# Loading the first q and k blocks as float32 pairs of blocks, and laying the steps anew

## The chip, the cores and the metric

The kernel runs on one core of a Trainium2 chip. The metric is the device time of one execution in microseconds (us). Instructions run on TensorE (PE, with its weight loads PEld), VectorE (DVE), ScalarE (ACT) and GpSimd (POOL); DMAs are issued by SyncE (SP), ACT and GpSimd.

## The reference

Sliding-window attention with a few global keys and a linear bias by distance, then a two-layer feed-forward network (FFN) with a softplus. Batch 4, 8 heads, 768 tokens, head size 64; 8 global keys, a window of 96; the FFN goes from 512 to 2048 and back to 512, over 3072 tokens.

```python
scores = scale * np.matmul(q, k.transpose(0, 1, 3, 2))
is_global = pos[None, :] < 8
is_local = (rel >= 0) & (rel < 96)
dist = np.where(is_global & ~is_local, 96.0, np.abs(rel))
scores = scores - slopes[:, None, None] * dist
scores = np.where(is_global | is_local, scores, -1e9)
a = softmax(scores)                     # with the row maximum taken off
x = np.matmul(a, v)                     # then heads side by side: (3072, 512)
h = x @ w_in
g = np.maximum(h, 0.0) + np.log1p(np.exp(-np.abs(h)))
out = g @ w_out
```

## The kernel before

The 3072 tokens are cut into 24 blocks of 128 (six to a batch) and 12 chunks of 256 for the FFN. A window of 96 reaches at most into the block before, so block n needs the keys and values of blocks n and n-1; the global keys of a batch's first block are copied over the first columns of the previous block's keys and values (gk and gv).

There is no loop that sets the order. A long string, ORDER, lists the steps one by one, each a short name with numbers, and KINDS maps a name to a function. Every engine runs its own instructions in the order in which the string emits them, so a step that waits holds up whatever its engine has behind it. A second string, BANKS, gives the PSUM bank (one of three) of each any_bank tile in the order of allocation.

The steps that matter here:

- lq, lk, lv: loads of a block's q, k, v by GpSimd's queue, from float32 in HBM to bf16 in SBUF. A single block is read in runs of 256 bytes (64 float32 of one head and token). For n in PAIRED (line 119), load_pair (line 124) reads two blocks in one DMA: partition s gets tokens 2s and 2s+1, in runs of 512 bytes. Before the change PAIRED holds 2 only.
- Block 0 is loaded differently (lines 87 to 92): as float32 into q_f by SP's queue and k_f by ACT's queue. cq (line 843) casts q to bf16 on DVE; ck (line 846) casts half of k on DVE and half on ACT.
- Transposes: t (line 275) of a block's q and k, four 128x128 transposes each; tq and tk (lines 851, 856) the same for block 0; tQ and tK (tr_pair, line 280) 16 half-width ones for the q or k of a pair. qc and kc copy the results from PSUM to QT and KT, on DVE, or on ACT when the last number is 1. For pairs these copies also interleave even and odd tokens. Later blocks are transposed by DMA (d).
- bb: parts of the bias table on ACT. z: the bias multiplied into PSUM by the identity, for blocks 0 to 3. s: the scores of half the heads, e: the exponential on ACT, p: the product with v, nm: the division on DVE, x and xc: the transpose to XT and its copy (y: by DMA).
- f, fe, lp, o: FFN of chunks 0 and 1, written as plain products. From chunk 2 on both layers use a seven-product scheme on quarters (h, hc, hv, he, hl; m, ec, ev, gs), with sums of weights made once (hw, wd). wi and wo load weights on GpSimd's queue. st stores by SP's queue.
- The last chunk's product m11.2 is cut in two column parts at LW (line 683); st11.0 is stored in the same two parts.
- g: a tiny copy on GpSimd that waits for a finished G, so that what stands behind it on GpSimd is issued later.

The beginning of ORDER before, in which w18 is 9 dummy matmuls that keep TensorE running until data is there:

```python
lk1 cq0 w18 bb1.0 lq1 z0.1 lq2 ck0 tq0 lv0 bb1.1 z0.0 tk0 s0.1 e0.1 lk2 s0.0 t1 kc1.0
lv1 qc1.0 lk4 z1.1 tQ2 s1.1 bb0.1 qc2.0 lq4 p0.1 e0.0 qc3.0 bb0.0 lv2 e1.1 p0.0 z1.0 wi1
```

Of the kernel before, what the change touches and what calls it, by code (L numbers as in the profile page):

```python
# [20 lines left out]
def kernel(  # L21
# [11 lines left out]
    nc = tc.nc  # L33
# [85 lines left out]
    PAIRED = (2,)  # L119
# [77 lines left out]
    def bias_part(half, part):  # L197
# [8 lines left out]
        "01201201022012012012012010120120120020012000102202001010200212201010222001102001"  # L206
        "122102021220110121210112020112020110"
# [475 lines left out]
    LW = 64  # L683
# [59 lines left out]
    def gate(s):  # L743
# [5 lines left out]
        lk1 cq0 w18 bb1.0 lq1 z0.1 lq2 ck0 tq0 lv0 bb1.1 z0.0 tk0 s0.1 e0.1 lk2 s0.0 t1 kc1.0  # L749
        lv1 qc1.0 lk4 z1.1 tQ2 s1.1 bb0.1 qc2.0 lq4 p0.1 e0.0 qc3.0 bb0.0 lv2 e1.1 p0.0 z1.0 wi1  # L750
        s1.0 lv3 nm0.0 tK2 e1.0 wi3 p1.1 lq5 gk2.1 lk5 wi0 nm0.1 kc2.0 p1.0 z2.0 z2.1 s2.1 x0
        s2.0 nm1.1 kc3.1 t4 gv2.0 gk3.0 nm1.0 e2.1 x1 z3.1 e2.0 lv4 wi2 qc4.1 z3.0 xc0.1 xc1.0
        s3.0 s3.1 kc4.0 p2.0 nm2.0 p2.1 nm2.1 f1 gv3.2 e3.0 p3.0 gk4.0 wi4 e3.1 x2 fe1 p3.1
        xc2.1 s4.0 gv4.1 f3 nm3.0 nm3.1 x3 ab4.0 t5 wo0 fe3 xc3.0 e4.0 s4.1 f9 lv5 ab4.1 kc5.1
        wi6 qc5.1 wo1 f11 fe9 e4.1 fe11 f8 gk5.2 f0 fe8 p4.0 s5.0 fe0 f10 ab5.0 lp0 nm4.0 hw1.0
        fe10 f2 s5.1 p4.1 f4 gv5.2 fe2 ab5.1 e5.0 f12 wo2 lp1 f5 o0 nm4.1 lq6 p5.0 hw2.0 o4 e5.1
        lk6 fe12 wo3 lk7 hw3.0 nm5.0 lq7 wd1.0 lp4 fe5 gv13 p5.1 fe4 x4 nm5.1 f13 xc4.0 x5 lp5
        hw3.1 fe13 f6 lp6 fe6 gs1.3 xc5.0 lq8 f14 f7 fe14 wd1.1 hw1.1 f15 h2.1.0 fe7 ht2.1 hw2.1
        o5 h2.5.0 fe15 lk8 ht2.2 hw4.1 lv6 lv7 hc2.1.0.1 ht2.4 hw4.0 h2.2.0 lp3 o1 lp2 h2.6.0
        wd3.0 o6 gv12 gk12 he2.11.0 hc2.5.0.0 wd2.0 lp7 hv2.6.0 wd4.0 ht2.3 gs1.1 t6 qc6.1 kc6.0  # L760
        h2.3.0 o2 o7 he2.12.0 hl2.0.0 wd3.1 lq9 os0.1.1 gs1.2 h2.7.0 ss6 t7 g7 hv2.7.0 ab6.0
        e6.0 o3 h2.4.0 os0.0.1 ac6.1 he2.21.0 qc7.0 kc7.0 lk9 wd2.1 ss7 ac6.0 gk8.2 m1.1.0 d8
        he2.22.0 ab7.0 e6.1 p6.0 h2.5.1 h2.1.1 ec1.1.1 lk11 hc2.5.1.1 ac7.0 hc2.1.1.1 lk10 g15
        e7.0 m1.6 nm6.0 p6.1 h2.2.1 lq10 h2.6.1 ec1.6.1 ac7.1 he2.11.1 m1.2.1 nm6.1 x6 p7.0
        wd4.1 hv2.6.1 h2.3.1 gs1.4 ev1.2 d9 e7.1 st0.1 nm7.0 xc6.1 h2.7.1 st0.0 hv2.7.1 ss8 d10
        gk9.2 he2.12.1 lv8 hl2.1.0 hl2.0.1 p7.1 ab8.0 m1.7 ac8.0 nm7.1 h2.4.1 h3.1.0 ec1.7.1
        lq11 m1.4 lv9 ac8.1 he2.21.1 hc3.1.0.1 x7 xc7.0 h3.2.0 gs2.3 ss9 e8.0 ec1.4.1 he3.11.0
        ht3.1 he2.22.1 e8.1 ac9.0 lq12 m1.5.0 ht3.2 ac9.1 ev1.5 h3.5.0 gv8.2 h3.6.0 lk12 p8.0
        ht3.4 m1.3 hc3.5.0.1 h3.1.1 ht3.3 hv3.6.0 nm8.0 d11 g21 e9.1 h3.3.0 ev1.3 p8.1 ab9.0
        hl2.1.1 he3.12.0 hc3.1.1.1 h3.7.0 m2.1.0 h3.2.1 e9.0 gk10.2 hv3.7.0 he3.11.1 nm8.1  # L770
        ec2.1.1 lv10 gv9.2 gs2.1 h3.4.0 p9.0 lq15 he3.21.0 h3.6.1 nm9.0 h3.5.1 hc3.5.1.1 p9.1
        hl3.0.0 lk13 ss10 gs2.2 he3.22.0 m2.6 gk11.2 nm9.1 hv3.6.1 h3.3.1 ec2.6.1 he3.12.1
        ab10.0 e10.0 y8 ac10.1 hl3.0.1 h3.7.1 y9 ac10.0 hv3.7.1 m2.7 d12 lv11 gv10.2 ec2.7.1
        ss11 p10.0 lq13 ac11.1 h4.1.0 h3.4.1 ac11.0 nm10.0 e10.1 ht4.1 m2.4 lk15 he3.21.1 ab11.0
        hc4.1.0.1 m2.2.1 h4.5.0 gs2.4 ht4.2 p10.1 gv11.0 ec2.4.1 ev2.2 he3.22.1 g27 m2.5.0 lq14
        ev2.5 lk14 hc4.5.0.1 d13 h4.6.0 ht4.3 hv4.6.0 e11.0 h4.2.0 hl3.1.0 he4.11.0 m2.3 h4.7.0
        ss12 nm10.1 ht4.4 p11.0 y10 ev2.3 lv13 hv4.7.0 nm11.0 e11.1 hl3.1.1 g23 d14 ac12.0 g13
        h4.3.0 gs3.1 ac12.1 h4.4.0 he4.12.0 p11.1 h4.1.1 m3.1.0 he4.21.0 hc4.1.1.1 gs3.2 nm11.1
# [64 lines left out]
    def cast_q(n):  # L843
        nc.vector.tensor_copy(q_t[n], q_f)
# [68 lines left out]
```

## Time and profile before

| | |
|---|---|
| Median of 3 runs | 201.0 us (200.4 to 202.69) |
| Profiled execution | 200.51 us |
| Its span, first to last instruction | 198.4 us |
| Instructions | 6719 |
| TensorE busy | 192.1 us (97%) |
| ScalarE busy | 175.2 us (88%) |
| VectorE busy | 172.7 us (87%) |
| GpSimd busy | 83.4 us (42%) |
| Mean granted TensorE clock | 0.998 |

Times in the profile count from the first instruction of the span. A group line gives line, engine and operation, output and inputs by the program's names, shapes and count, then busy time and the mean length of one. In the timeline each row has a start, a length, the engine and its line; brackets at the end hold the engine's idle time just before and what ended it. Matmuls are pipelined, so the lengths of neighbours overlap, and what a step costs is better read from one start to the next.

### The profile page before, as it was taken

The numbers are of one execution on the slowest core, as the hardware profiler recorded it, in microseconds if no ns is written. First come the engines' busy times: TensorE is split into PE (matmuls) and PEld (weight loads), VectorE is DVE, ScalarE is ACT, GpSimd is POOL, SyncE is SP. The second block draws the span as 40 slices with busy tenths as digits, with TensorE's granted clock in tenths as the row PEclk, the third lists the DMA queues.
The fourth block names the chain that finished last, engine by engine and source line by source line (L and its number), as shares of the span: only waits on it lengthen the run. The fifth ranks groups of instructions, "written<-read, shape, count | busy, mean of one in ns | idle before, by whom it ended". The sixth has DMA issues, their size and how long they took to land.

```text
span 198.4 us, 6719 instructions
## 1 busy us (share of the span) xinstructions
PE 192.1 (97%) x2743; PEld 167.6 (84%) x2745; DVE 172.7 (87%) x404; ACT 175.2 (88%) x283; POOL 83.4 (42%) x134
## 2 busy tenths in 40 slices
PE   8889999999999989999999999999999999999993
PEld 3557887867988979999999998999999999999992
DVE  7576578999999999999999999999979998896551
ACT  2779999997999999999999999999999999976900
POOL 8997439532395675175469138235011100000000
PEclk9999999999999999999999999999999999999999
DMA  8999999999999999999999959999945111403123
GB/s 131 162 169 175 197 198 207 188 158 150 181 93 112 165 135 155 151 194 183 131 165 168 160 131 130 167 175 197 83 106 83 30 44 48 125 3 107 56 90 122
DMA packets 108542, 26.91 MB, mean 136 GB/s; under 512 B 99680, under 2 KB 106208, under 8 KB 108512
## 3 DMA queue, kind: packets, MB, share of 16 engines
q0 software_dynamic: 76000, 13.37, 99.3%
q1 hardware_dynamic: 31472, 12.85, 36.8%
q8 instruction: 21, 0.34, 0.7%
q10 hardware_dynamic: 1040, 0.26, 0.6%
q14 instruction: 9, 0.07, 0.1%
HBM read 27.26 MB, written 6.29 MB: 169 GB/s over the span
## 4 chain that ended last, share of the span: by engine, by line
PE 86%; DMA 6%; POOL 2%; DVE 2%; issue 1%; ACT 1%; POOLq 0%; ACTq 0%
PE o L698 33%; PE hT L582 22%; PE p_ps L582 8%; PE hT L475 7%; PE x_ps L421 5%; PE o L627 3%; PE s_ps L325 3%; DMA XT<-xsf 3%; DMA v_t<-in_v_dram 3%; PE s_lo L325 1%; ACT Pb L405 1%; PE tr L241 1%; PE tr_x L454 1%; DVE Z L394 1%; POOL k_t L103 1%
## 5 line engine op out<-in xcount | busy, mean ns | idle before, releaser
L616 ACT ACTIVATE G<-e_sb 128x1024 f16<-128x1024 f32 x40 | 42.2, 1064 | 0.1
L405 ACT ACTIVATE Pb<-Z 128x1024 bf16<-128x1024 f32 (+1 forms) x40 | 40.0, 1002 | 1.4 <-DVE Z L383 1.2
L582 PEld LDWEIGHTS <-w_sum 128*128 128x128 f16 x640 | 39.0, 98 | 1.8 <-issue 0.2
L698 PEld LDWEIGHTS <-sum 128*128 128x128 f16 x352 | 32.5, 98 | 3.9 <-issue 0.2
L698 PE MATMUL o<-w_dif,sum 128*128 128x256 f16 x264 | 33.9, 273 | 0.0
L582 PEld LDWEIGHTS <-w_in 128*128 128x128 f16 x480 | 29.2, 98 | 1.6 <-DMA XT<-xsf 0.7
L698 PEld LDWEIGHTS <-G 128*128 128x128 f16 x272 | 24.8, 98 | 2.7
L385 DVE TENSOR_TENSOR Z<-s_ps,biasA 128x1024 f32<-128x1024 f32 x19 | 23.1, 1216 | 3.2 <-PE s_ps L325 3.2
L582 PE MATMUL hT<-XT,w_in 128*128 128x128 f16 x320 | 24.4, 219 | 0.6 <-DMA XT<-xsf 0.6
L612 ACT ACTIVATE e_sb<-hT 128x512 f32<-128x512 f32 x40 | 24.0, 604 | 1.0 <-PE hT L582 0.7
L582 PE MATMUL hT<-x_dif,w_sum 128*128 128x128 f16 x320 | 24.4, 219 | 0.1
L103 POOL DMA_DIRECT2D v_t<-in_v_dram x24 | 21.3, 888 | 4.6 <-issue 2.1
L698 PE MATMUL o<-w_out,G 128*128 128x256 f16 x168 | 21.8, 273 | 0.0
L316 POOL COPY v_t<-v_t 8x520 bf16<-8x520 bf16 x11 | 7.2, 652 | 31.0 <-PE x_ps L421 29.6
L439 DVE TENSOR_TENSOR xsf<-x_ps,rcp 128x256 f16<-128x256 f32 x44 | 18.7, 424 | 1.5
L103 POOL DMA_DIRECT2D k_t<-in_k_dram x21 | 18.8, 895 | 1.1 <-DMA w_out<-in_moe_w_out_dram 0.8
L103 POOL DMA_DIRECT2D q_t<-in_q_dram x21 | 18.7, 893 | 1.1 <-issue 1.1
L421 PE MATMUL x_ps<-v_t,Pb 128*128 128x65 bf16 x324 | 17.1, 193 | 0.0
L421 PEld LDWEIGHTS <-Pb 128*128 128x128 bf16 x352 | 15.1, 97 | 2.3 <-issue 0.6
L668 DVE TENSOR_TENSOR sum<-G 128x1024 f16<-128x1024 f16 x22 | 15.1, 685 | 0.5 <-ACT G L616 0.4
L475 PE MATMUL hT<-XT,w_in 128*128 128x256 f16 x128 | 15.2, 273 | 0.0
L607 DVE TENSOR_TENSOR p_ps<-hp,hT 128x512 f32<-128x512 f32 x20 | 13.8, 690 | 1.2 <-ACT hp L595 0.6
(123 smaller groups left out, 385.0 us busy)
## 6 DMA issues: line engine op xcount, KB each, us to landing
out_dram<-osb SPq DMA_DIRECT2D x18, 256.0 KB, 4.1
v_t<-in_v_dram POOLq DMA_DIRECT2D x24, 128.0 KB, 5.8
k_t<-in_k_dram POOLq DMA_DIRECT2D x21, 128.0 KB, 5.5
q_t<-in_q_dram POOLq DMA_DIRECT2D x21, 128.0 KB, 6.3
w_out<-in_moe_w_out_dram POOLq DMA_DIRECT2D x4, 512.0 KB, 9.8
out_dram<-osb SPq DMA_DIRECT2D x10, 128.0 KB, 1.9
w_in<-in_moe_w_in_dram POOLq DMA_DIRECT2D x4, 256.0 KB, 7.3
w_in<-in_moe_w_in_dram POOLq DMA_DIRECT2D x2, 512.0 KB, 9.7
```

Source lines behind the costliest of these rows:

```text
L103: nc.gpsimd.dma_start(dst[n][:, :, 0:D], src[b, :, i * P : (i + 1) * P, :].rearrange("h s d -> s h d"))
L385: nc.vector.tensor_tensor(Z[:], buf[:, 0:8, :], biasA[:, half, :, :], ALU.add)
L405: nc.scalar.activation(Pb[:, 0:nreg, :], src, AF.Exp, scale=inv_sqrt)
L421: nc.tensor.matmul(x_b[:, lh, :], Pb[:, r, :], v_t[n - t][:, h, :], start=(t == 0), stop=(t == 1 or first),)
L439: nc.vector.tensor_tensor(xsf[:, h0 : h0 + 4, :], x_b[:, :, 0:D], rcp[:, h0 : h0 + 4][:, :, None].to_broadcast([P, 4, D]), ALU.mult,)
L475: nc.tensor.matmul(hT[:, j, :], w[:, m, fo : fo + P], XT[c][:, m, :], start=(j == 0 and m == 0), stop=(m == KM - 1), skip_group_check=(j > 0),
L582: nc.tensor.matmul(o[:, b, :], lhs(k, b), rhs[:, k, :], start=(i in (1, 5) and b == 0 and k == 0), stop=(k == KH - 1), skip_group_check=True,)
L607: nc.vector.tensor_tensor(t, HS[c, "p", u][:], HT[c, "x", u][:], ALU.add)
L612: nc.scalar.activation(o, t, AF.Exp)
L616: nc.scalar.activation(g_tile(c)[:, b0 : b0 + HB, :], HS.pop((c, i, u))[:], AF.Ln, bias=1.0)
L668: sum_by(by)(SM[c, i][:], a(), b(), op)
L698: nc.tensor.matmul(o, lhs[:, k, :], rhs(k)[:, c0:c1], start=(i in (1, 2, 5) and k == 0), stop=(k == NU - 1), skip_group_check=(i not in (1 ...
```

## The change

PAIRED becomes (0, 2, 4). The float32 loads of block 0 become float32 loads of blocks 0 and 1, 512 KB each, in runs of 512 bytes, so lq1 and lk1 are gone from GpSimd's queue; cq and ck cast twice as much. Blocks 4 and 5 are loaded as a pair by GpSimd, so lq5 and lk5 are gone. tq0, tk0, t1, t4 and t5 are replaced by tQ0, tK0, tQ4 and tK4, with two more copies, qc0 and kc0. LW goes from 64 to 128. ORDER and BANKS are rewritten throughout; beside the order, several PSUM evictions and small copies change engine.

```diff
-        work.tile([P, 8, P], F32, tag="Z", name=name)[:, 0:4, :].rearrange("p a (x d) -> p (a x) d", d=D)
+        work.tile([P, 8, P], F32, tag="Z", name=name)[:].rearrange("p a (x d) -> p (a x) d", d=D)
...
-    nc.sync.dma_start(q_f, q[0, :, 0:P, :].rearrange("h s d -> s h d"))
-    nc.scalar.dma_start(k_f, k[0, :, 0:P, :].rearrange("h s d -> s h d"))
+    for queue, t_f, src in ((nc.sync, q_f, q), (nc.scalar, k_f, k)):
+        queue.dma_start(
+            t_f.rearrange("p (h t) d -> p h t d", t=2),
+            src[0, :, 0 : 2 * P, :].rearrange("h (s t) d -> s h t d", t=2),
+        )
...
-    PAIRED = (2,)
+    PAIRED = (0, 2, 4)
...
-    LW = 64
+    LW = 128
...
-        lk1 cq0 w18 bb1.0 lq1 z0.1 lq2 ck0 tq0 lv0 bb1.1 z0.0 tk0 s0.1 e0.1 lk2 s0.0 t1 kc1.0
-        lv1 qc1.0 lk4 z1.1 tQ2 s1.1 bb0.1 qc2.0 lq4 p0.1 e0.0 qc3.0 bb0.0 lv2 e1.1 p0.0 z1.0 wi1
...
+        lk2 w18 cq0 bb0.0 ck0 lq2 z0.1 tQ0 tK0 bb0.1 lk4 qc0.0 lv0 lv1 bb1.1 z0.0 kc0.0 kc1.0
+        tK2 qc1.1 s0.0 kc3.0 e0.0 lq4 s0.1 e0.1 tQ2 z1.0 bb1.0 s1.0 tK4 z1.1 lv2 s1.1 wi1 e1.0
+        qc2.0 e1.1 p0.0 kc2.0 gk2.2 kc5.1 nm0.0 wi0 p0.1 z2.0 s2.0 p1.0 z2.1 nm0.1 s2.1 lv3 p1.1
+        nm1.0 wi2 kc4.1 qc3.0 gk12 tQ4 nm1.1 e2.0 e2.1 gv2.0 x0 xc0.1 z3.0 wi3 qc5.0 gk3.0 x1
+        p2.0 qc4.0 z3.1 p2.1 s3.0 nm2.0 nm2.1 s3.1 xc1.1 wi4 lk6 gv3.0 e3.0 e3.1 gk4.0 f1 lv4
+        s4.0 fe1 ab4.0 wi6 x2 xc2.1 f0 fe0 p3.1 nm3.1 wo1 e4.0 p3.0 s4.1 gk5.1 nm3.0 lv5 f2 x3
...
-        m10.3 ec11.1.1 st8.0 st9.0 gs11.1 m11.2.2.1 st10.1 m11.2.2.0 gs11.2 m11.6 ev10.3
-        ec11.6.0 m10.2.1 gs11.4 ev10.2 m11.7 m11.5.1 st10.0 ec11.7.1 ev11.2.0 m11.4 ev11.5
-        ec11.4.1 ev11.2.1 st11.0.1 st11.1 m11.3 ev11.3 st11.0.0
...
+        m11.2.2.0 m10.3 gs11.3 ec11.1.1 st8.0 m11.6 ec11.6.1 ev10.3 st9.0 st10.1 gs11.4 m10.2.1
+        ev11.2.0 ev10.2 m11.7 ec11.7.1 m11.5.1 m11.4 st10.0 ev11.5 m11.3 m11.2.2.1 ec11.4.1 gk13
+        st11.1 ev11.3 st11.0.0 ev11.2.1 st11.0.1
...
     def cast_q(n):
-        nc.vector.tensor_copy(q_t[n], q_f)
+        nc.vector.tensor_copy(q_p[n // 2][:], q_f)
 
     def cast_k(n):
-        half = H // 2
-        nc.vector.tensor_copy(k_t[n][:, 0:half, :], k_f[:, 0:half, :])
-        nc.scalar.copy(k_t[n][:, half:H, :], k_f[:, half:H, :])
-
-    def tr_first_q(n):
...
-    def tr_first_k(n):
...
+        nc.vector.tensor_copy(k_p[n // 2][:, 0:H, :], k_f[:, 0:H, :])
+        nc.scalar.copy(k_p[n // 2][:, H : 2 * H, :], k_f[:, H : 2 * H, :])
```

gk and gv do something only for blocks 2 to 5 of a batch; gk12 and gk13 emit nothing.

More of the change, by code (lines that the diff above doesn't have):

```diff
@@ L205 @@
     BANKS = iter(
-        "01201201022012012012012010120120120020012000102202001010200212201010222001102001"
-        "122102021220110121210112020112020110"
+        "01201221020120120210102102102120101010121212012212020212121000121210002211120012"
+        "21210102202122101120101212001221001"
     )
@@ L748 @@
     ORDER = """
-        lk1 cq0 w18 bb1.0 lq1 z0.1 lq2 ck0 tq0 lv0 bb1.1 z0.0 tk0 s0.1 e0.1 lk2 s0.0 t1 kc1.0
-        lv1 qc1.0 lk4 z1.1 tQ2 s1.1 bb0.1 qc2.0 lq4 p0.1 e0.0 qc3.0 bb0.0 lv2 e1.1 p0.0 z1.0 wi1
[L751 to L754, printed above, removed]
```

162 lines of the change are left out of this document (78 added, 84 removed).

## The prediction
> **What bounds the kernel now.** I read the page's busy shares first, then TensorE by stretches (columns: length, then PE, PEld, DVE, ACT, POOL busy with counts, granted clock, DMA share, GB/s), then the longest TensorE wait in the timeline.
>
> ```profile
> PE 192.1 (97%) x2743; PEld 167.6 (84%) x2745; DVE 172.7 (87%) x404; ACT 175.2 (88%) x283; POOL 83.4 (42%) x134
> 22.00:190.00 168.00, 167.20 (x2447) 150.70 (x2446) 154.60 (x339) 158.73 (x255) 63.70 (x106) 1.00 1.38 134
> 72.17 0.62 PE L582 MATMUL hT<-XT,w_in 128*128 128x128 f16 x8 [0.60 <-DMA XT<-xsf]
> ```
>
> From 22 to 190 us TensorE stands still for 0.8 us in 168 (167.20 busy), most of it one wait of 0.60 for a DMA transpose. The body can give back at most that; anything larger must come from the start or the end. In the start "busy" tells little, because the first 4 us are dummy matmuls. There the chain that ended last is the view to read:
>
> ```profile
> 5.96 5.63 DMA v_t<-in_v_dram
> ...
> 13.66 0.61 ACT Pb L405
> ...
> 17.39 0.87 PE hT L475 x8
> ...
> 25.28 0.33 PE s_ps L325 x8
> ```
>
> The path runs through GpSimd's issues into the landing of block 1's v at 11.59, through two exponentials, to the first FFN product near 17.3 us. Before that product TensorE has too little to do; after it, there is always filler.
>
> **The start as it is.** Timeline of the instructions that the change moves, in order of time (start, length, engine, line):
>
> ```profile
> 0.78 4.00 PE L841 MATMUL x_ps<-const-bfloat16-1.0 128*128 128x512 bf16 x9 [0.78 <-PEq L894]
> 4.86 0.43 DVE L844 CAST q_t<-q_f 128x512 bf16<-128x512 f32 x1
> 5.22 0.27 DVE L848 CAST k_t<-k_f 128x256 bf16<-128x256 f32 x1
> 5.34 0.61 PE L241 MATMUL tr<-ident,q_t 128*128 128x128 bf16 x4
> 5.47 0.39 ACT L849 CAST k_t<-k_f 128x256 bf16<-128x256 f32 x1
> 6.73 0.42 DVE L260 COPY KT<-tr_k 128x512 bf16<-128x512 bf16 x1 [0.32 <-PE tr_k L241]
> 7.54 0.60 ACT L405 ACTIVATE Pb<-oo 128x512 bf16<-128x512 f32 x1 [1.06 <-PE oo L325]
> 7.54 0.40 PE L241 MATMUL tr<-ident,q_t 128*128 128x128 bf16 x4
> 8.71 0.64 PE L286 MATMUL tr_q<-ident,q_t 128*64 128x128 bf16 x16
> 9.12 0.72 ACT L199 ACTIVATE biasA<-dist_dp 128x256 bf16<-128x256 bf16 x2
> 9.39 1.29 DVE L292 COPY QT<-tr_q 128x512 bf16<-128x512 bf16 x2 [0.43 <-PE tr_q L286]
> 9.42 0.80 POOL L109 DMA_DIRECT2D w_in<-in_moe_w_in_dram  x1
> 12.40 0.58 ACT L292 COPY KT<-tr_k 128x512 bf16<-128x512 bf16 x1 [0.42 <-DVE KT L292]
> 13.66 1.02 ACT L405 ACTIVATE Pb<-oo 128x1024 bf16<-128x1024 f32 x1 [0.68 <-PE oo L325]
> 14.58 1.02 ACT L405 ACTIVATE Pb<-s_ps 128x1024 bf16<-128x1024 f32 x1
> 15.49 0.59 ACT L253 COPY QT<-tr 128x512 bf16<-128x512 bf16 x1
> 15.95 0.62 ACT L461 COPY XT<-tr_x 128x512 f16<-128x512 f16 x1
> 17.22 1.03 PE L475 MATMUL hT<-XT,w_in 128*128 128x256 f16 x8
> 17.60 1.02 ACT L405 ACTIVATE Pb<-oo 128x1024 bf16<-128x1024 f32 x1
> 21.36 3.68 PE L475 MATMUL hT<-XT,w_in 128*128 128x256 f16 x32
> ```
>
> Three things are to be seen. ACT waited 1.06, 0.42 and 0.68 us between its early steps. And neighbours overlap: exponentials at 13.66 and 14.58 start 0.92 apart though each lasts 1.02, the copies at 15.49 and 15.95 are 0.46 apart, the two biases at 9.12 are followed after 0.61. I step by these distances. And TensorE begins slow: nine products of 512 columns in 4.00 us are 0.44 apiece, while eight of 256 columns later take 0.87; four transposes take 0.61 at 5.34 and 0.40 at 7.54. The clock rises between these two.
>
> **The landing of the float32 pairs.** The trace has no 512-byte load by SP's or ACT's queue, so its time is bounded (queue lines and issue lines of 0 to 6 us, stretches, last two stores, and the landing of the weight load issued at 9.42):
>
> ```profile
> q10 hardware_dynamic: 1040, 0.26, 19.4%
> q_f<-in_q_dram SPq DMA_DIRECT2D x1, 256.0 KB, 3.6
> k_f<-in_k_dram ACTq DMA_DIRECT2D x1, 256.0 KB, 4.3
> out_dram<-osb SPq DMA_DIRECT2D x1, 224.0 KB, 1.9
> out_dram<-osb SPq DMA_DIRECT2D x1, 32.0 KB, 1.5
> 3.00:4.00 1.00, 1.00 (x4) 0.32 (x3) 1.00 (x9) 0.00 (x0) 1.00 (x2) 1.00 1.23 274
> DMA to landing us min/median/max: 5.9/5.9/5.9
> 16.00:17.00 1.00, 1.00 (x27) 0.72 (x26) 0.42 (x1) 0.89 (x3) 0.00 (x0) 1.00 1.74 181
> ```
>
> Both issues are at 0.74, so q_f lands at 4.3 and k_f at 5.0 before. The packets stay 1040 a tensor and double in size. If the packet sets the price, nothing moves: 4.3 and 5.0. If bytes set all beyond the 1.5 us of the smallest store, q_f needs 1.5 + 2 x 2.1 and k_f 1.5 + 2 x 2.8: landings 6.4 and 7.8. At the 274 GB/s that these loads reach themselves, the added 0.52 MB costs 1.9 us; half of it has passed when q_f is done. I take 5.9 and 6.7, near that row.
>
> The Trainium skill (DMA: Bandwidth & Descriptors, Queues, rings and completion order) says each DMA engine alternates between the queues that have work. By it GpSimd's first pair would cut into k_f's tail and k_f would land near the upper bound; the sum below would rise by about 0.4. The trace has both queues at work between 4 and 5 us, no more.
>
> **The change part by part.** (1) The q cast doubles: 0.43 plus twice the 0.16 that 256 more columns cost (0.43 against 0.27) is 0.75, at 5.95 to 6.7. The k cast is split as now, 0.43 on DVE and 0.58 (the row of a 512-column ACT copy) on ACT, where it holds up the biases behind it: ACT idles from 5.6 to 6.75.
> (2) Each pair of one tensor takes 16 half-width transposes (0.64 at 8.71) for eight full ones (two times the 0.40 at 7.54, which overlap): between 0 and 0.2 us more for each of four pairs, I take 0.1. All lie before the first FFN product, where TensorE has room. The interleaved copies of a pair take 1.29 for two, 0.6 from start to start, where a plain one takes 0.42 (6.73); DVE sat waiting for such transposes (0.32 and 0.43 in the brackets), so it has the time. Without that room each would push the keys by 0.2 to 0.3.
> (3) So queries at 7.4 to 8.1, keys 8.0 to 8.7, first scores at 8.75 and the first exponential at 9.05, 1.5 later than 7.54. From there ACT hardly waits: second exponential 9.5, last bias 9.95, e1.0 10.6, e1.1 11.75 (its scores stand behind the transposes of block 4's keys, the third load on GpSimd's queue), two key copies 12.7 and 13.1, e2 13.6 and 14.5, the XT copies 15.4 and 15.9, e3.0 16.4, e3.1 17.3. Before, e3.1 starts at 17.60. The three waits of 2.2 us pay for the late start, and blocks 4 and 5 are already transposed, which before falls partly after that point (block 5: some 0.5 of TensorE and two ACT copies).
> (4) The first FFN product: XT is ready at 16.5. Its weights landed at 9.42 + 5.9 = 15.3. Ahead of them on GpSimd's queue stand two pairs and seven single loads before, four pairs and three singles after, equal in bytes; the hardware queues put up to 1.9 us more in front, and half the packets give some back. I take +1.3 of 0 to 1.9: 16.6. The third product's weights come three loads later (0.64 MB written at 181 GB/s, 3.5 us): about 20.2; the fourth's 1.4 later, 21.6.
> (5) Count of work: before, the four products from 21.36 end at 25.04, six in all. After: f1 16.75, f0 near 18.2, block 3's outputs, f2 at 20.2, f3 at 21.6, block 5's scores, then three products by 25.4, seven in all and block 5's scores (0.33) done. One product is 0.87. That is 0.87 + 0.33 ahead, less 0.3 for the later clock: **-0.9 us**. GpSimd loses four issues (0.8 to 1.0 each); DMA data, not issue, sets its landings, so I give nothing for them.
> (6) Gains a wait: gk2 moves from ACT to GpSimd and waits there for block 1's second scores (near 11.7). Behind it queue wi0, lv3, wi2, wi3. At 12.0 wi0 still lands by about 17.9 with the 5.9 of the row above; f0 at 18.2 is just covered.
> (7) The body: exchanges of copies between ACT and DVE nearly cancel (eight output copies to DVE, six back). The transpose that TensorE awaits at 72.17 is issued earlier among its neighbours, right after block 8's second norm; half of its 0.60 counts, **-0.3**, because the new order can have its own such wait (bounds -0.8 to +1.5).
> (8) The end:
>
> ```profile
> 193.78 0.21 DVE L737 TENSOR_TENSOR osb<-a,o_end 128x64 f32<-128x64 f32 x1
> 194.06 1.04 PE L698 MATMUL o<-w_out,sum 128*128 128x256 f16 x8
> 195.13 0.42 DVE L737 TENSOR_TENSOR osb<-b,o 128x256 f32<-128x256 f32 x1 [1.14 <-PE o L698]
> ```
>
> Before, the last matmuls feed a 256-column sum and a 224 KB store. Afterwards 128 columns are left for the last eight matmuls: the 256-column sum and a 192 KB store begin about 0.43 earlier beside them, and a sum of about 0.27 and a 64 KB store come last. That is 0.15 on DVE and 0.3 of the 0.4 between the two store rows: **-0.4** (bounds -0.45 and 0).
>
> **Sum.** The profiled execution took 200.51 us, 2.1 outside its span of 198.4. 200.51 - 0.9 - 0.3 - 0.4 = 198.9; I say 199.0, 1.0% under the median of 201.0 (the profiled one lay 0.5 below that).
>
> **Rivals.**
> - Packets set the price: q_f lands by 4.5 and k_f by 5.2. DVE's setup holds its casts until 4.86 anyway, so step 3 starts about 1.4 earlier, while the weights hold f2; about half reaches TensorE: 198.2. It needs no other step to differ. For it: 128-row stores of seven times the bytes take 0.4 longer. Against it: 274 GB/s was the fastest second of the start. The Trainium skill (DMA: Bandwidth & Descriptors, Specifications) has transfers under 512 B pay extra and 512 B at line rate, which would be this rival; the 256-byte packets here prove neither.
> - Nothing gained at the start. Either both landings are at the upper bound and the weights 1.9 later: f1 moves to about 17.7, f2 to 20.8, the 0.9 is gone, 199.8 to 200.5. Or TensorE's clock rises late: the dummies end at 4.8 as before, but what follows them comes at 6.7 instead of 5.34, so the slow rate may last through the first transposes and scores, 0.2 to 0.3 on each of four steps of the chain and as much again if it lasts to block 1: 199.9 to 200.9. The Trainium skill (TensorE: Matmul & The Clock Gate, What's actually happening) describes such a clock, raised by a sustained busy window of about 3.4 us and lowered by an idle one; the trace agrees with the rise, and no run here shows the fall.
> - Slower: GpSimd's order. Block 4's key pair is late, so the transposes ahead of block 1's second scores hold TensorE, those scores hold gk2, and gk2 holds wi0, lv3, wi2 and wi3. It decides once those scores end after 12.3 us; at 14.3, from pairs landing some 2 us apart, the weights move by 2 to 2.5 and f0, f2 and f3 wait for them, which turns -0.9 into about +2; with the end's -0.4 that is 202.1, and up to 203.5 where the later weights are held too. For it: block 1's v needed 5.63 from issue to landing. Against it: ACT itself would not take those scores before 11.5.
>
> **How the numbers follow.** Forecast 0.48 (198.2 to 199.8), cheap packets 0.12, no gain 0.27 (199.8 to 200.9), slower 0.13. Over 1% (2 us, about what a measurement of this kernel can tell from no change) faster than 201.0 means under 199.0: a bit over half of the forecast and the first rival, 0.40. Slower by that much, over 203.0, takes half of the last rival: 0.07. The rest is 0.53. The range leaves out the tails of the first and last rival: 198.0 to 202.0.
>
> **What would show it.** k_f's landing at 6.2 to 7.2 and the first exponential near 9.05; no ACT wait over 0.5 us between 9 and 17 us; f1 before 17.2; seven products of 1.03 by 25.5; GpSimd's gk2 before 12.3. The forecast is wrong if f1 is later than 17.2, if the body of 22 to 190 us idles over 1.5 us, or if the last store lands more than 2.9 us after the last matmul.

## The result, and the profile after

The changed kernel is slower: 203.58 us as the median of 20 executions (201.66 to 206.62) against 201.12 (200.32 to 202.69), a ratio of 1.011 (95% interval 1.0089 to 1.0132). The medians count all executions, while the ratios leave out those in a slower state of the chip (2 of the 20 here), so a ratio can lie beside the quotient of two medians. Predicted were 199.0 and a range of 198.0 to 202.0. The profiled execution took 203.94 us, with a span of 202.2. That is 3.4 above the profiled execution before (200.51), more than the medians differ.

The page of the changed kernel, its busy shares and its clock by fortieths of the span, then its stretches (length, PE, PEld, DVE, ACT, POOL busy with counts, granted clock, DMA share, GB/s):

```profile
PE 192.8 (95%) x2774; PEld 168.2 (83%) x2777; DVE 175.5 (87%) x406; ACT 175.8 (87%) x279; POOL 78.2 (39%) x132
...
PEclk9699999999999999999999999999999999999999
```

```profile
5.00:10.00 5.00, 2.71 (x40) 2.13 (x42) 3.32 (x6) 2.98 (x8) 3.48 (x4) 0.70 1.71 201
...
20.00:75.00 55.00, 55.00 (x757) 46.41 (x755) 50.70 (x110) 52.49 (x84) 29.22 (x42) 1.00 1.82 174
75.00:170.00 95.00, 92.63 (x1449) 84.83 (x1447) 89.76 (x203) 91.28 (x144) 35.28 (x70) 1.00 1.31 122
```

The kernel before has this in the first and the last of these stretches:

```profile
5.00:10.00 5.00, 4.32 (x62) 2.97 (x62) 2.70 (x14) 3.94 (x12) 5.00 (x6) 1.00 1.98 162
...
75.00:170.00 95.00, 95.00 (x1498) 88.24 (x1496) 91.70 (x207) 93.05 (x151) 35.38 (x65) 1.00 1.38 132
```

Two places stand out. From 5 to 10 us TensorE is busy for 2.71 of 5 us at a granted clock of 0.70, where before it was 4.32 at 1.00. And from 75 to 170 us, where the kernel before never stands still, TensorE is idle for 2.37 us.

The start, in the timeline of the changed kernel, row by row as the prediction stepped through it:

```profile
4.08 0.38 PE L349 MATMUL oo<-bias,ident 128*128 128x256 bf16 x2
6.08 1.16 DVE L847 CAST q_t<-q_f 128x1024 bf16<-128x1024 f32 x1 [1.06 <-DMA q_f<-in_q_dram]
6.94 0.62 ACT L851 CAST k_t<-k_f 128x512 bf16<-128x512 f32 x1 [1.39 <-DMA k_f<-in_k_dram]
7.16 0.78 DVE L850 CAST k_t<-k_f 128x512 bf16<-128x512 f32 x1
7.29 1.06 PE L289 MATMUL tr_q<-ident,q_t 128*64 128x128 bf16 x16 [2.83 <-DVE q_t L847]
8.15 1.06 PE L289 MATMUL tr_k<-ident,k_t 128*64 128x128 bf16 x16
9.68 0.96 PE L289 MATMUL tr_k<-ident,k_t 128*64 128x128 bf16 x16
10.57 0.28 PE L328 MATMUL s_ps<-QT,KT 64*128 64x128 bf16 x4
10.89 0.60 ACT L408 ACTIVATE Pb<-s_ps 128x512 bf16<-128x512 f32 x1 [1.19 <-PE s_ps L328]
13.86 0.21 POOL L315 COPY KT<-KT 128x32 bf16<-128x32 bf16 x1 [5.38 <-PE oo L328]
13.94 1.02 ACT L408 ACTIVATE Pb<-oo 128x1024 bf16<-128x1024 f32 x1 [0.41 <-PE oo L328]
19.38 1.02 ACT L408 ACTIVATE Pb<-s_ps 128x1024 bf16<-128x1024 f32 x1 [0.64 <-PE s_ps L328]
19.43 1.05 PE L478 MATMUL hT<-XT,w_in 128*128 128x256 f16 x8
21.02 1.04 PE L478 MATMUL hT<-XT,w_in 128*128 128x256 f16 x8
```

q_f was cast from 6.08 and k_f from 6.94, so the loads came as forecast (5.9 and 6.7). Everything behind them is late, and by more at each step: the q cast takes 1.16 us, the transposes begin at 7.29 after 2.83 us of idle TensorE and take 1.06 instead of 0.64 for sixteen, the first exponential is at 10.89 instead of 9.05, and the first FFN product at 19.43 instead of 16.75.

The body, in the changed kernel's timeline: the issues of DMA transposes on SP's queue and the two longest waits that they end.

```profile
79.75 1.21 SPq L273 DMA_TRANSPOSE QT<-q_t  x1
81.06 1.65 SPq L274 DMA_TRANSPOSE KT<-k_t  x1
82.94 1.19 SPq L453 DMA_TRANSPOSE XT<-xsf  x1
...
90.03 0.29 DVE L556 TENSOR_TENSOR x_dif<-XT 128x256 f16<-128x256 f16 x1 [1.24 <-DMA XT<-xsf]
90.38 0.62 PE L585 MATMUL p_ps<-x_dif,w_sum 128*128 128x128 f16 x8 [0.84 <-DVE x_dif L556]
...
117.55 1.24 SPq L274 DMA_TRANSPOSE KT<-k_t  x1
...
123.83 0.29 PE L328 MATMUL s_ps<-QT,KT 64*128 64x128 bf16 x4 [0.76 <-DMA KT<-k_t]
```

Both chains hang on a transpose by DMA. The one issued at 82.94 is used by DVE at 90.03 as soon as it is there; the one issued at 117.55 is used by TensorE at 123.83. The chain of work that ended last names the same two:

```profile
82.94 7.07 DMA XT<-xsf
...
117.55 6.24 DMA KT<-k_t
```

The end, in the changed kernel's timeline:

```profile
198.48 0.61 PE L701 MATMUL o_end<-w_out,G 128*128 128x128 f16 x8
198.68 0.42 DVE L740 TENSOR_TENSOR osb<-b,o 128x256 f32<-128x256 f32 x1 [1.27 <-PE o L701]
199.12 0.29 DVE L740 TENSOR_TENSOR osb<-a,o_end 128x128 f32<-128x128 f32 x1
```

The last matmul ends at 199.09, 3.07 us ahead of the span's end; before it was 195.09 and 3.34.

To place the loss I counted, from the start times of all matmuls in each trace, when the same amount of TensorE work is done (output columns without the dummies and the transposes, since the two kernels do these differently; 2400 columns are called one us of work). The table gives how much later than the kernel before each kernel reaches that amount, in us; the kernel before is there at 32, 76, 142 and 186 us. The rows below the first are those of the experiments. Each row is one trace, and most traces caught a faster execution than the median, so the second column has both times. Traces lack a few matmuls (the counts of the two kernels differ by 0.2 us of work), so a row is good to about 0.2.

| kernel | traced execution (median) | 20 us of work | 60 | 125 | 168 |
|---|---|---|---|---|---|
| changed | 203.94 (203.58) | 1.8 | 0.6 | 3.7 | 4.2 |
| changed, 21 dummies | 202.0 (203.1) | 0.7 | -0.7 | 2.2 | 2.3 |
| old start, new rest | 203.15 (204.2) | 0.8 | 0.2 | 2.9 | 3.0 |
| new start, old rest | 202.4 (203.58) | 2.8 | 2.2 | 2.3 | 2.3 |
| pairs in the old order | 207.36 (209.8) | 7.2 | 7.1 | 7.1 | 7.1 |
| new start with 21 dummies, old rest | 204.97 (206.53) | 0.1 | -0.7 | 4.0 | 4.0 |
| changed, without loads of blocks 12 to 23 | 201.14 (201.16) | 1.4 | 0.0 | 0.6 | 0.8 |
| before, without these loads | 199.81 (199.81) | 0.3 | -1.0 | -0.9 | -0.8 |
| changed, two steps moved | 201.58 (202.17) | 2.1 | 0.8 | 1.7 | 1.9 |
| edited start, two steps moved | 203.49 (204.82) | 1.0 | -0.4 | 3.7 | 3.8 |
| edited start, three steps moved | 201.51 (201.7) | 0.9 | -0.4 | 1.7 | 1.8 |
| edited start, four steps moved | 203.04 (201.57) | 0.9 | -0.4 | 3.3 | 3.3 |

So in the first row the start costs 1.8, the middle gives 1.2 back (from 20 to 75 us TensorE idles 0.80 us in the kernel before, and not at all in the changed one), and the body from there on costs 3.6, of which 2.37 are idle time. The last matmul ends 4.0 later than before, and the end gives 0.27 back, which leaves the 3.7 between the spans.

### The profile page after: what moved, and what is told of

Its sections match the earlier page's. It is cut to its first block, busy times and chain, and to the rows that moved or that the text cites. A ratio compares the mean times of both kernels' runs of the same rounds, so it can differ in the third digit from the quotient of the medians.

```text
span 202.2 us, 6753 instructions
## 1 busy us (share of the span) xinstructions
PE 192.8 (95%) x2774; PEld 168.2 (83%) x2777; DVE 175.5 (87%) x406; ACT 175.8 (87%) x279; POOL 78.2 (39%) x132
## 4 chain that ended last, share of the span: by engine, by line
PE 53%; DVE 22%; DMA 17%; ACT 2%; issue 2%; POOL 1%; DVEq 0%; POOLq 0%
PE o L701 17%; PE hT L585 10%; DMA XT<-xsf 9%; PE hT L478 7%; PE p_ps L585 5%; DVE Z L397 4%; DVE Z L388 3%; DMA KT<-k_t 3%; PE o L630 3%; DVE xsf L442 3%; DMA q_f<-in_q_dram 3%; DVE sum L671 3%; PE x_ps L424 2%; PE s_ps L328 2%; DMA q_t<-in_q_dram 2%
## 5 line engine op out<-in xcount | busy, mean ns | idle before, releaser
L106 POOL DMA_DIRECT2D q_t<-in_q_dram x18 | 15.9, 886 | 5.4 <-DMA w_in<-in_moe_w_in_dram 3.0
L106 POOL DMA_DIRECT2D k_t<-in_k_dram x18 | 16.0, 888 | 2.3 <-DMA v_t<-in_v_dram 1.1
```

Of the source, the lines that this page charges most:

```text
L106: nc.gpsimd.dma_start(dst[n][:, :, 0:D], src[b, :, i * P : (i + 1) * P, :].rearrange("h s d -> s h d"))
```

## The experiments

**The clock of the start.** The changed kernel with 21 dummy matmuls instead of 9, so that TensorE isn't idle before the first transposes.

```diff
-        lk2 w18 cq0 bb0.0 ck0
+        lk2 w42 cq0 bb0.0 ck0
```

> The changed kernel with 21 dummy matmuls at the start instead of 9, enough to keep TensorE running until the q pair has landed and been cast. Clock theory: TensorE's clock fell in the 2.8 us gap ahead of the first transposes (1.06 us for 16 instead of 0.64), so now all four groups of transposes take 0.64, the first exponential starts near 9.9 us instead of 10.89, the first FFN product near 18.4 instead of 19.43, and the time falls by about 1.0 to 202.6. Rival, the landing alone: the clock is not what delays the chain, the first FFN product moves by under 0.3 and the time stays within 0.3 of 203.6.

Measured: 203.1 us, ratio 1.0101 (1.0067 to 1.0136). Its stretch from 5 to 10 us, and three rows of its timeline:

```profile
5.00:10.00 5.00, 4.77 (x77) 2.87 (x77) 3.87 (x7) 3.09 (x9) 3.48 (x4) 1.00 1.70 203
```

```profile
7.29 0.64 PE L289 MATMUL tr_q<-ident,q_t 128*64 128x128 bf16 x16 [0.16 <-DVE q_t L847]
...
9.79 0.60 ACT L408 ACTIVATE Pb<-s_ps 128x512 bf16<-128x512 f32 x1 [0.50 <-PE s_ps L328]
...
18.32 1.05 PE L478 MATMUL hT<-XT,w_in 128*128 128x256 f16 x8
```

The transposes start at the same 7.29 but take 0.64, and everything behind is 1.1 us earlier (9.79 against 10.89, 18.32 against 19.43). The slow pace after the idle stretch is 1.1 us of this start, as the clock theory said. The time is another matter: the median fell by 0.5 and the ratio by 0.001, less than the interval can tell from nothing, and 203.1 lies between the theory's 202.6 and its rival's 203.3. The trace, the fastest of nine executions, keeps the gain to the end (2.3 against 4.2 in the table); where the slower executions lost it no trace shows.

How much a start pays for the pace differs from one execution to the next. The kernel with two steps moved, further down, has the same start with 9 dummies, and its trace has this:

```profile
7.29 0.64 PE L288 MATMUL tr_q<-ident,q_t 128*64 128x128 bf16 x16 [2.09 <-DVE q_t L842]
...
9.03 1.06 PE L288 MATMUL tr_k<-ident,k_t 128*64 128x128 bf16 x16
...
10.46 0.60 ACT L407 ACTIVATE Pb<-s_ps 128x512 bf16<-128x512 f32 x1 [1.18 <-PE s_ps L327]
```

There the first transposes behind the gap run at full pace, and the pace falls near 8.6, when TensorE is already at work again. In the trace of the new start with the old rest, below, every matmul up to 12.2 is slow, dummies included. In four traces with this start and 9 dummies the first exponential comes between 10.46 and 11.13; in none of the eight with 16 or 21 dummies does TensorE fall back to the slow pace once it has left it. So the 1.1 is the price in one trace and not a fixed one.

**The start and the rest, each alone.** The old start with the new order, banks and end behind it, and the new start with the old ones (cut at step t6; a step that would be missing or come twice is put in or left out at the seam). A third kernel keeps the old order and has only the pairs' loads and transposes.

```diff
# old start, new rest: ORDER of before up to t6, then that of after; LW = 128
# new start, old rest: ORDER of after up to t6, then that of before; LW = 64
# pairs in the old order: ORDER of before with
-lk1 cq0 w18 bb1.0 lq1 ... tq0 ... tk0 ... t1 ...
+w18 cq0 bb1.0 ... tQ0 ... tK0 ... (lq1, lk1, lq5, lk5 gone; tQ4, tK4 for t4, t5)
```

> The kernel before up to the transposes of block 6 (loads, single blocks and order as before), and from there the new order with its banks and its end. Order theory: the waits for DMA transposes belong to the new body, so TensorE still idles some 3 us between 75 and 170 us; without the 1.9 us of the new start the time is about 201.7. Rival, the late start makes the body late: with the old start those waits fall to the 1.3 us of before, and with the new end's 0.4 the time is about 200.5.

> The changed kernel up to the transposes of block 6, and from there the order of before with its banks and its end. Start theory: the first 40 us cost 1.9 us more than before and nothing later gives it back, the body waits 1.3 us as before: about 203.0. Rival, the body takes the delay up (ACT and DVE are ahead there): about 201.2 to 201.8.

> The order and banks of before with the new loads alone: q and k of blocks 0 and 1 as float32 pairs, of 4 and 5 as pairs, the pair transposes in the places of the single ones, block 5's copies moved up beside block 4's; the old body and end. If the pairs' late landing and the slow clock are the loss, the start is as late as in the changed kernel or later (first FFN product 19 to 20 us) and the time 203 to 204. Rival, the new order made the loss: the pairs alone cost under 0.5, 201.5.

Measured: 204.2 us (1.0151; 1.0098 to 1.0205), 203.58 (1.0123; 1.0059 to 1.0186) and 209.8 (1.0391; 1.0311 to 1.0472). Both halves cost time by themselves. The new start is within 0.6 of its theory (203.0). The old start is 2.5 above the order theory (201.7) and further above the rival; its trace idles 1.87 us from 75 to 170, where the theory had some 3, and 1.46 of that in one wait for KT. The third is far above both its forecasts. The old start varies by 0.8 from one trace to another (its first GpSimd load landed at 6.33 instead of 5.51 us), so a start is known to about that. In the third kernel ACT waits 2.48 us for the first scores, and sixteen transposes still take 1.06 at 15.64:

```profile
6.74 1.07 PE L288 MATMUL tr_q<-ident,q_t 128*64 128x128 bf16 x16 [1.53 <-DVE q_t L842]
...
10.57 0.60 ACT L407 ACTIVATE Pb<-oo 128x512 bf16<-128x512 f32 x1 [2.48 <-PE oo L327]
...
15.64 1.06 PE L288 MATMUL tr_k<-ident,k_t 128*64 128x128 bf16 x16
```

So the start with the pairs in the old order is 7.2 us late, and the new order of the first steps wins most of that back. How much of the 7.2 the pairs alone cost isn't shown: in this trace TensorE is at the slow pace from the first dummy to 16.4, while in the changed kernel's it is back at full pace by 10.4.

**Is it the new body's order, or any body that comes early?** The new start with 21 dummies and the old rest.

> The new start with 21 dummy matmuls, then the body and end of before. The parts as found so far: the new start with the clock kept up costs about 0.8, the old body and end nothing: 201.7. Rival, the new start delays the body by more than TensorE's own lateness shows (as the new start on the old body, 203.6, hints): over 202.5.

Measured: 206.53 us (1.0288; 1.0238 to 1.0338), far above the first theory and in the rival's range. Its start is level with the kernel before (0.1 at 20 us of work), and it loses 4.7 us between 60 and 125:

```profile
145.13 0.40 PE L327 MATMUL s_ps<-QT,KT 64*128 64x128 bf16 x8 [2.50 <-DMA KT<-k_t]
```

So the old order can have long waits too behind another start. It need not: behind the new start with 9 dummies its trace shows TensorE busy for all 95.00 us from 75 to 170. Twelve more dummies, which bring the first exponential of this kernel forward, made it slower (1.0288 against 1.0123). So where a transpose comes too late hangs on when the body begins too, and not on its order alone.

**The loads taken away.** Both kernels without the loads of q, k and v of blocks 12 to 23; these blocks compute on what lies in their buffers.

```diff
-lk12 lq12 lv12 ... lk23 lq23 lv23
```

> The changed kernel without GpSimd's loads of q, k and v for blocks 12 to 23: these blocks work on what is left in the buffers (that part of the input is left out). Backlog theory: the body's waits are DMA transposes of x, q and k that take 6 to 7 us because loads stand in front of them on the same DMA engines; without the loads a transpose lands in about 3 us and TensorE's idle time between 75 and 170 us falls from 2.4 us to under 0.8; time about 201.5. Rival, SP's queue or the producers are late (divisions on DVE, SP's issue order): the waits stay and the time stays within 0.7 of 203.6.

> The kernel before with the same loads left out (blocks 12 to 23 work on old data), as the control. Backlog theory: its order left the transposes enough time, its body waits after 75 us are near nothing, so at most 0.4 is gained: about 200.6. Rival, the missing loads speed up something else that both kernels share: it gains as much as the changed kernel does.

Measured: 201.16 us (1.0006; 0.9978 to 1.0034) and 199.81 (0.993; 0.9904 to 0.9956). The changed kernel comes out as the backlog theory said (201.5). The control gained 0.7%, 1.4 us, where at most 0.4 was expected, so part of the gain has nothing to do with the new order. The landing of the transposes to XT in the changed kernel, without the loads, and then with them:

```profile
DMA to landing us min/median/max: 2.4/2.5/4.1
```

```profile
DMA to landing us min/median/max: 2.4/4.7/7.1
```

```profile
75.00:170.00 95.00, 94.83 (x1491) 87.62 (x1489) 91.17 (x207) 93.59 (x149) 11.14 (x39) 1.00 0.43 87
```

Without the loads the median transpose needs 2.5 us instead of 4.7, and TensorE's idle time in this stretch (this row is the changed kernel's without loads) is 0.17 us instead of 2.37. The transposes to XT are as slow in the kernel before as in the changed one (2.4/4.6/8.2 in the same view), those to QT and KT faster (medians of 5.2 and 5.0 against 6.4 and 6.2). So for XT it is not the speed that changed, but the time that the order leaves, which the moved steps below test. What is left between the two kernels without loads, 1.35 us, is in the table 1.1 of the start and 0.5 of the body, less the end.

**The end alone.** The kernel before with the last 69 steps and the LW of the changed one; one step of the body, h4.1.0, also stands behind h3.4.1, so that the wait at 72.17 has work in front of it.

```diff
-    LW = 64
+    LW = 128
-... h4.1.0 ... h3.4.1 ... (last 69 steps of before)
+... h3.4.1 h4.1.0 ... (last 69 steps of after)
```

> The kernel before with the end of the changed one (LW 128 and its last 69 steps), and the product of block 8 that waited 0.6 us for its DMA transpose put one product (0.45 us) later. End theory: last matmul to end of span falls from 3.3 to about 2.9 us (-0.4), and the wait shrinks to about 0.15 (-0.45): about 200.3, faster than both. Rival: the store of 192 KB that starts earlier ends last all the same, and the moved product only moves the wait: within 0.2 of 201.

> The kernel before with the changed kernel's last 69 steps and its 128-column last piece, without the loads of blocks 12 to 23. Theory: the end is worth the 0.4 us that was predicted: 199.4 us against 199.81. Rival: the last store's landing does not shrink with its size and only the 0.15 on DVE is left: 199.65; or nothing, 199.8.

Measured: 201.56 us (1.0013; 0.9984 to 1.0043), and not the 200.3 of the end theory. In its trace 3.05 us lie behind the last matmul instead of 3.34, but a wait of its own took the gain:

```profile
179.53 0.61 PE L581 MATMUL p_ps<-x_dif,w_sum 128*128 128x128 f16 x8 [0.58 <-ACT e_sb L611]
```

Without the loads, and with h4.1.0 where it was, 200.26 (0.993; 0.9903 to 0.9957), the same ratio as without the new end; the gap in that place (0.58 at 178.07) is there again. The end's gain could not be had by itself.

**The pieces of the start, with the loads away.** Three kernels: 21 dummies; these and the q cast split; the old start with the new rest.

```diff
# 21 dummies: w42 for w18; and with the split cast
-        nc.vector.tensor_copy(q_p[n // 2][:], q_f)
+        nc.vector.tensor_copy(q_p[n // 2][:, 0:H, :], q_f[:, 0:H, :])
+        nc.scalar.copy(q_p[n // 2][:, H : 2 * H, :], q_f[:, H : 2 * H, :])
```

> The changed kernel with 21 dummy matmuls instead of 9 and without the loads of q, k and v of blocks 12 to 23, so those blocks compute on what lies in their tiles. The same without the extra dummies took 201.16 us. Theory: TensorE's clock after its idle stretch is 1.1 us of what the new start costs, so 200.1 us (199.8 to 200.4), with the 16 transposes of the first pair in 0.64 and no wait over 0.3 us in the body. Rival: with the loads away the later first exponential alone sets the start, and the clock does not matter: 200.9 to 201.3.

> As the kernel with 21 dummies and without the loads of blocks 12 to 23, but the cast of the first q pair is split by blocks between DVE and ACT as that of k is. Theory: the cast of 1.16 us is the first step of the chain; half of it ends about 0.4 earlier (DVE's half 0.78), so the transposes start near 6.9, and 0.3 to 0.4 us comes off: 199.7 us if the unsplit one has 200.1. Rival: the next step waits for something else, k's landing at 6.9 or the third pair ahead of the first scores, and the time stays at 200.0 to 200.2 although the transposes of q start earlier.

> The start of the kernel before, then the order and the end of the changed one, without the loads of blocks 12 to 23. The kernel before without these loads took 199.81 us. Theory: the new order costs nothing by itself, only through transposes that stand behind loads, so what is left is the new end: 199.5 us (199.3 to 199.7). Rival: the new order costs TensorE time of its own even where no transpose is late: 200.3 or more.

Measured: 200.89 us (0.9972; 0.9941 to 1.0004), 200.6 (0.9962; 0.9923 to 1.0001) and 200.68 (0.9951; 0.992 to 0.9982). The clock's 1.1 did not come through whole: by the ratios 0.7 us came off, on the edge of the rival's range, and in its trace a gap of 0.73 us stands at 134.60, because DVE waited for a store to free an output buffer. The split helped nothing that can be measured; its transposes were held until 8.36 by the dummies, which in that trace stayed at the slow pace until about 6 and so lasted to 8.2. The old start missed its theory (199.5) and is in the rival's range (200.3 or more), but it has a gap of 0.53 at 45.76, at the seam, so it says little of the order itself.

**Two steps of the body moved.** In the changed kernel d15 (transposes of block 15, whose scores come 93 steps later) stands right ahead of y11 on SP's queue, while before it stood 20 steps behind; d18 stands 20 steps ahead of its scores (step 700 and 720), where before there were 54.

```diff
-... gs3.4 d15 y11 ac13.0 ...          -... g39 gs5.1 d19 ... hc7.1.0.1 m5.7 d18 p17.0 ...
+... gs3.4 y11 d15 ac13.0 ...          +... g39 gs5.1 d18 d19 ... hc7.1.0.1 m5.7 p17.0 ...
```

> The changed kernel with two steps of its order moved and nothing else: the DMA transposes of block 15's q and k stand behind the transpose y11 instead of right ahead of it, and those of block 18 stand ahead of block 19's instead of 44 steps behind. Theory: the two long TensorE waits of the changed kernel (near 90.4 and 123.8 us, 1.0 and 0.9) come from this order on SP's queue, where a transpose that is needed soon stands behind one that is needed late; both go and the time falls by 1.5 to 1.9, to 201.7 to 202.1 us, with TensorE waits in 75 to 170 us of 0.5 in all instead of 2.4. Rival: the loads on the same DMA engines make transposes late whatever their order; other waits take their place and the time stays at 203.0 to 203.6.

Measured: 202.17 us, 1.0056 (1.002 to 1.0092) of before, close to the theory's 201.7 to 202.1. That is 1.4 below the changed kernel by the medians and 1.1 by the ratios. Its stretch:

```profile
75.00:170.00 95.00, 94.78 (x1483) 87.17 (x1482) 91.04 (x206) 93.31 (x148) 37.02 (x70) 1.00 1.29 128
```

The two waits are gone and none came in their place: 0.22 us idle instead of 2.37, with all loads there. In the table the body's loss from 60 us of work on falls from 3.6 to 1.1. This is the clearest of the runs: two positions in the order make most of the body's loss in the traces. By the times, whose intervals still touch, they are about half of the whole loss of 1.1%.

**An edited start.** 16 dummies, the split cast, and block 0's keys copied by ACT, with one bias behind that copy; once without the loads, once with them and the two moved steps.

```diff
-        lk2 w18 ... qc0.0 lv0 lv1 bb1.1 z0.0 kc0.0 kc1.0
+        lk2 w32 ... qc0.0 lv0 lv1 z0.0 kc0.1 bb1.1 kc1.0
```

> The changed kernel without the loads of blocks 12 to 23 (they compute on what lies in their tiles), and with three edits of its start: 16 dummies instead of 9, the cast of q split between DVE and ACT, and block 0's keys copied by ACT with one bias put behind that copy. The kernel with 21 dummies and none of the other edits had its first exponential at 10.1 and took 200.9 us, 0.997 of before. Theory: the casts and DVE's row of copies are the chain of the start; the first exponential comes at 9.2 to 9.6 and the time is 0.5 to 0.7 lower: 200.2 to 200.4. Rival: the landings behind (block 1's v, the weights) set the first FFN product, and the time stays at 200.7 to 201.0 although the first exponential is earlier.

> The changed kernel with its loads, the three edits of the start (16 dummies, split cast of q, block 0's keys by ACT) and the two moved steps of the body. Theory: 1.1 for the clock, 0.5 for the casts and copies and 1.5 to 1.9 for the two waits come off 203.6: 200.2 to 200.6 us, 0.995 to 0.998 of the kernel before. Rival: an earlier start meets the same loads and store queue earlier, and what it gains comes back as waits in the body: 201.6 to 202.5.

Measured: 200.97 us (0.9993; 0.9969 to 1.0017), in the rival's range and not the theory's, and 204.82 (1.0192; 1.0162 to 1.0222), above both forecasts. The first, in its timeline:

```profile
9.07 0.72 ACT L202 ACTIVATE biasA<-dist_dp 128x256 bf16<-128x256 bf16 x2
9.37 0.29 PE L327 MATMUL s_ps<-QT,KT 64*128 64x128 bf16 x4
...
9.70 0.57 ACT L294 COPY QT<-tr_q 128x512 bf16<-128x512 bf16 x1
...
10.16 0.61 ACT L407 ACTIVATE Pb<-s_ps 128x512 bf16<-128x512 f32 x1
```

The first scores end near 9.65, but ACT has a bias and a copy of queries ahead of the exponential, which comes at 10.16, no earlier than the 10.13 with 21 dummies alone. My edit had put that bias there. The second lost 4.1 us between 60 and 125 us of work. Its timeline there:

```profile
129.99 1.21 SPq L272 DMA_TRANSPOSE QT<-q_t  x1
131.30 1.21 SPq L273 DMA_TRANSPOSE KT<-k_t  x1
...
132.56 2.87 SPq L713 DMA_DIRECT2D out_dram<-osb  x4
...
135.77 0.42 DVE L739 TENSOR_TENSOR osb<-a,o 128x256 f32<-128x256 f32 x1 [1.84 <-DMA out_dram<-osb]
```

DVE waits for a store to free an output buffer, for 1.84 us; the store was issued behind the transposes of block 23, which stand 37 steps ahead of st5.0 in this order (in the kernel before they stand 92 behind). TensorE then stands still for 1.71 at 137.05.

**A third step moved**, d23 behind st5.0, with the edited start and with the changed kernel's own:

```diff
-... he7.22.0 d23 hc7.5.1.1 ... hl7.1.0 h8.6.0 st5.0 nm18.1 ...
+... he7.22.0 hc7.5.1.1 ... hl7.1.0 h8.6.0 st5.0 d23 nm18.1 ...
```

> The kernel with the edited start and the two moved steps (204.8 us), with one more step moved: the DMA transposes of block 23's q and k, which stand 40 steps ahead of the output stores of token chunks 4 and 5 on SP's queue, go behind them. Theory: the wait of 1.7 to 1.9 us near 137 comes from DVE waiting for an output buffer whose store stands behind those transposes; it goes, and the time is 202.7 to 203.2 us. The wait of 0.9 near 100 stays. Rival: the store is late because the transposes and loads hold the DMA engines, not because of its place on the queue; then the wait moves to another place and the time stays at 204.4 to 205.0.

> The changed kernel with the two moved steps and the same third one, and the start as changed. Its profile without the third move had no wait of that kind. Theory: what is left against the kernel before is the start alone, less the end: 201.8 to 202.2 us. Rival: the third move helps in those executions that the profile did not catch: 201.2 to 201.7; or it brings a wait of its own, for block 23's keys: above 202.5.

Measured: 201.7 us (1.0003; 0.9979 to 1.0027) and 203.42 (1.0046; 1.0003 to 1.0089). With the edited start 3.1 us came off, more than the wait itself and more than forecast; the theory of the queue's order holds in direction, and the gap at 100 went too in that trace, which I can't put down to the moved step. With the changed kernel's own start the third move gave nothing that can be measured (1.0046 against 1.0056) and missed its theory (201.8 to 202.2); nine of its ten executions spread from 201.03 to 203.92.

**A fourth**, d20 behind y16 and y17, since y16 was issued 2.6 us after its input was ready:

```diff
-... ev4.3 ... d20 ... y16 ... y17 ...
+... ev4.3 ... y16 ... y17 d20 ...
```

> The kernel with the edited start and three moved steps (201.7 us, 1.000 of before), with a fourth: the DMA transposes of block 20's q and k go behind y16 and y17 instead of 7 steps ahead of them. In its profile y16 is issued at 126.5 although its input was ready at 123.9, because KT of block 20 held SP's queue from 123.9 to 126.4; TensorE then waits near 130.9 and 131.8 (1.2 in all, with DVE's two differences between). Theory: the order on SP's queue is the cause again; these waits go and the time falls by 0.9 to 1.2, to 200.5 to 200.8 us, 0.994 to 0.996 of the kernel before. Rival: block 20's keys become late in their turn, or a transpose of that stretch is late wherever it stands: 201.4 to 202.2.

Measured: 201.57 us (1.0017; 0.9988 to 1.0046), in the rival's range: nothing gained. The waits near 131 are gone in its profile, but that execution (203.04) has a wait elsewhere, for a transpose issued by the same order as in the kernel with three moves:

```profile
101.30 0.62 PE L584 MATMUL hT<-XT,w_in 128*128 128x128 f16 x8 [1.78 <-DMA XT<-xsf]
```

No version beat the kernel before. The best are level with it.

## Why the prediction was wrong, step by step

Two steps failed: the start, which was to gain 0.9 and lost 1.8, and the body, which was to gain 0.3 and lost 2.4. All three of the prediction's signs of being wrong came up: f1 at 19.43 (limit 17.2), 2.37 us of idle TensorE from 22 to 190 (limit 1.5), and 3.07 us from the last matmul to the end (limit 2.9).

- **The landings** (5.9 and 6.7) were right: 6.05 and 6.91 in the trace. Cheap packets, the first rival, did not happen. The Trainium skill (DMA: Bandwidth & Descriptors, Specifications) has 512 bytes as the size from which a transfer goes at line rate; loads of 256-byte runs landed at 4.36 and 4.99 here, twice the bytes in 512-byte runs 1.7 and 1.9 later, about the 1.9 that the added bytes cost at 274 GB/s, so no large step of that kind is to be seen.
- **Step 1, the casts, failed in size.** The q cast took 1.16 and not 0.75, the k cast on DVE 0.78 and not 0.43. I had extrapolated from the difference of two casts that ran at another time. The length is not fixed by the columns: the same q cast took 0.69 in the trace with pairs in the old order and 0.99 to 1.16 in seven others; half of it took 0.43 on DVE in one trace and 0.89 in another. The cause is open.
- **Step 2 failed by the clock.** The prediction had TensorE slow "through the first transposes" only in a rival, with 199.9 to 200.9; it is what happened, and it cost 1.1 us at the first exponential, inside that rival's price (0.9 to 1.9 above the forecast). That the size came out right is partly luck, since the slow stretch lies elsewhere in other traces of the same start. The prediction kept 0.64 for sixteen transposes although it had the dummies ending at 4.8 and their successors at 6.7.
- **Step 3 failed from there.** 10.89 is 1.84 late. Of this 1.1 is the slow pace, by the 21 dummies, and some 0.4 is the length of the q cast. e1.1 is 2.2 late, e3.0 3.0 late. How the 0.7 beside the clock is split among casts, copies and ACT's order is only argued, since no run that made the casts shorter began its exponentials earlier.
- **Steps 4 and 5.** The weights were no limit: f1 waited for its data until 19.43, not for a landing. In place of seven products by 25.4 the fifth begins at 25.21. The -0.9 became +1.8.
- **Step 6.** gk2 ran on GpSimd at 13.86, beyond the 12.3 at which the slower rival was to decide, because block 1's scores came late. But its price was not paid: w_in's second part landed at 18.24, ahead of f0's turn at 21.02. The late start covered it. That the time of 203.58 lies next to this rival's 202.1 to 203.5 is luck.
- **Step 7 is the larger failure.** I gave the body -0.3 with bounds of -0.8 to +1.5; it was +2.4 after 20 us of work. TensorE's two waits behind DMA transposes are 1.6 of it (0.84 and 0.76); shorter waits make up the rest of the 2.37 of idle time. The prediction looked for the wait that the change takes away (the 0.6 at 72.17) and not at the slack that the new order leaves each other transpose. That could be read from the order and the trace of before together: steps between d and its scores, and what stands ahead on SP's queue. Moving two steps took the idle time from 2.37 to 0.22 and 1.1 to 1.4 us off the time.
- **Step 8**, the end's -0.4, was 0.27 by the time from the last matmul to the end (3.34 to 3.07). Put into the kernel before, it gained nothing in the time.

Not settled: why the same order waits at different places from one execution to another (the changed kernel spreads over 5 us, and over 2 without the loads), and with that how much of the waits any one order would keep. The pace of the start may be one source: in the four traces named above the first FFN product begins between 19.43 and 20.40; what that does to the time isn't shown. The moves treat the waits that a profile caught.

## What to carry to other kernels

When an order is laid anew, count for every transfer how many steps stand between its issue and its use and what stands ahead of it on its queue, in the old order and in the new: a wait that is gone in one place says nothing of the others. Put transfers that are used soon ahead of those that are used late, and stores that free a buffer ahead of transposes of far blocks. And if a change moves the first data later, ask what TensorE does in the gap: an idle stretch can be paid again in the pace of what follows.

## What the runs showed of the hardware

- In the changed kernel 2.83 us without a matmul were enough for TensorE to be back at the slow pace: sixteen transposes in 1.06 against 0.64. The Trainium skill (TensorE: Matmul & The Clock Gate, What's actually happening) gives an idle window of about 3.4 us, free-running; the gap here is shorter. With the same start and two steps moved, the gap was 2.09 us, the transposes behind it took 0.64, and the pace fell 1.3 us after TensorE had begun again. So the gap alone doesn't set where the slow stretch lies.
- The granted clock doesn't tell the pace: it was 0.70 from 5 to 10 us in the changed kernel, and 1.00 in the kernel with pairs in the old order, whose sixteen transposes took 1.07 in the same stretch.

```profile
5.00:10.00 5.00, 2.81 (x35) 1.78 (x34) 2.59 (x11) 1.81 (x5) 5.00 (x7) 1.00 1.86 194
```

- The DMA transposes to XT, from SBUF to SBUF, took a median of 2.4 and 2.5 us from issue to landing (at most 4.4) in the two kernels without GpSimd's later loads, and of 4.6 and 4.7 (up to 8.2 and 7.1) with them. Taking the loads away cut the spread of the executions of the kernel before to 0.65 us (199.35 to 200.0).
